# One 128-row read of a head's sums, and the clamp of the weight conversion on GpSimd, in a fused attention and mixer kernel

## The chip, the core and the metric

The kernel runs on one core of one Trainium2 chip. The metric is device time in microseconds (us), here from one launch to its end, as the median of several runs. The engines are named as the profile names them: PE is TensorE, PEld its weight loads, DVE is VectorE, ACT is ScalarE, POOL is GpSimd, SP is SyncE, from whose queue nearly all transfers are issued.

## The reference, cut to what matters

The inputs are q, k and v of shape (8, 8, 576, 64), batch, heads, rows, width, a projection `w_phi` of 64 x 128, and four weights of a mixer in float64. Attention is linear, with 256 features; the mixer works over tokens and then over channels.

```python
def phi(x):
    proj = np.einsum('bhsd,df->bhsf', x, w_phi)
    proj = proj - np.max(np.abs(proj), axis=-1, keepdims=True)
    return np.concatenate([np.exp(proj), np.exp(-proj)], axis=-1)
q_p, k_p = (phi(q), phi(k))
kv = np.einsum('bhsf,bhsd->bhfd', k_p, v)
z = np.sum(k_p, axis=2)
num = np.einsum('bhsf,bhfd->bhsd', q_p, kv)
den = np.einsum('bhsf,bhf->bhs', q_p, z)[..., None] + 1e-06
attn = num / den
...
h = np.maximum(xt @ w_tok1, 0.0) @ w_tok2
u = x + h.transpose(0, 2, 1)
h2 = np.maximum(u @ w_ch1, 0.0) @ w_ch2
return (u + h2).astype(np.float32)
```

## The kernel before, in words

**Streams and the order.** The work is written as five streams: keys (`keys`, line 672), queries (`queries`, 789), the token mix (`token_stream`, 1014), the load and conversion of the mixer's weights (`load_weights`, 568) and the channel mix (`channel_stream`, 1021). Every operation is recorded by a stand-in for the engine (so all of them carry line 175 in the profile), `weave` (1047) gives each a rank, and `arrange` (274) places them: it keeps a clock for each engine, takes the duration of an operation from `cost` (198), adds a lag for its readers, and writes down for each engine one fixed order. On the chip an engine goes through its own list in that order and waits on semaphores. The planner also knows that VectorE and GpSimd can hold each other up (`held`, `choose` at 259): an operation of VectorE that touches no PSUM (`shut`) is placed as if it had to wait for a running operation of GpSimd. GpSimd's operations are costed at 190 ns and 2.1 ns a column.

**Attention.** Heads go in pairs, 32 pairs for the 8 batches; pair i holds two heads j = 0 and 1. The rows of a head are cut into two segments k, of 320 and 256 rows (`SEG`). The first 7 pairs (`PLAIN`) are multiplied in plain f32, the rest in three products of split halves. `less_max` (615) projects, takes the largest absolute value of a row and subtracts it; for split pairs it copies one half out of PSUM (`part`), adds the other into `p` on VectorE, reduces, and lets GpSimd subtract. `turn` (823) transposes the result with TensorE into one PSUM tile `pt` of three blocks of 128 columns and takes the exponentials (`qf`, `qh`, `ql`).

**The numerators.** `numerators` (850) multiplies them with the keys' sums into a PSUM tile `pn` of 128 rows: for head j the 64 rows from 64 j on are the numerator, the other 64 rows are the denominator, one value repeated. Both are read out separately: ScalarE copies the numerator's rows into the attention's result `xt` (`x`), and the denominator's rows go, with 1e-6 added, into `den`, by ScalarE for the first 7 pairs and by VectorE for the other 25. For k = 0 and j = 1 the columns lie in another order, so that each of the two reads is split in two (`runs`). After j = 1 the denominators go through memory: two rows to `row`, back as a small tile `few`, VectorE's reciprocal, out to `inv`, and back by two transfers that repeat each row over 64 partitions of `den`; then GpSimd multiplies `xt` by `den`, in place. The branch for `i >= EARLY` is never taken, as there are 32 pairs and `EARLY` is 32. `den` has two buffers; three `rest` banks of PSUM are shared by `pt`, `pn` and others.

**The conversion.** `convert` (542) makes two f32 halves of a piece of float64 weights, 31 pieces in all, 24 of them 128 x 512 (`bitsc`, `wc`). ScalarE takes the absolute value of the upper word into `m`, VectorE clamps it, shifts it, and joins sign and lower bits in two more operations, ScalarE rounds to the upper half, GpSimd subtracts for the lower half. `m` comes from a ring of three buffers (`bits`). The token weights (7 pieces) come first, the channel weights (24 pieces) after.

**The mixer.** `token_mix` (903) transposes `xt` (`px`), multiplies (`pa`, `ph`) and adds back; `up_proj` and `down_proj` (971, 986) multiply with the channel weights (`h`, `acc`), and `leave` adds and stores.

Of the kernel before, what the change touches and what calls it, by code (L numbers as in the profile page):

```python
# [8 lines left out]
F32 = mybir.dt.float32  # L9
F32R = mybir.dt.float32r  # L10
U32 = mybir.dt.uint32
I64 = mybir.dt.int64
AF = mybir.ActivationFunctionType
ALU = mybir.AluOpType
# [3 lines left out]
P = 128  # L18
B, H, S, D = 8, 8, 576, 64
NP = H // 2  # L20
F = 128
# [4 lines left out]
PLAIN = 7  # L26
OPEN = 4
EARLY = 32
# [449 lines left out]
def mixer_kernel(ctx, tc, qk, qkp, vals, w_phi, w1, w1t, w2, wc1, wc2d, out):  # L478
# [41 lines left out]
    eps = odd.tile([P, 1], F32, tag="eps", name="eps", bufs=1)  # L520
    nc.gpsimd.memset(eps, 1e-6)
# [20 lines left out]
    def convert(hi, lo, src, name, tag=None):  # L542
# [13 lines left out]
        nc.vector.tensor_scalar(m.bitcast(F32), m.bitcast(F32), LEAST, MOST, op0=ALU.max, op1=ALU.min)  # L556
# [58 lines left out]
    def less_max(ts, units, name, base=None):  # L615
# [21 lines left out]
        if base is None:  # L637
            part = wk.tile([P, 2, F], F32, tag="part", name=f"part{name}")
            nc.scalar.copy(part[:, :n], ps[:, :n, 1])
            pr = wk.tile([P, 2, F], F32, tag="p", name=f"p{name}")  # L640
            nc.vector.tensor_tensor(pr[:, :n], ps[:, :n, 0], part[:, :n], op=ALU.add)
            pr, eng = pr[:, :n], nc.gpsimd
        else:
            pr, eng = ps[:, :n, 0], nc.vector
        mx = odd.tile([P, 2], F32, tag=f"mx{kind}", name=f"mx{name}")
# [177 lines left out]
    def turn(i, k, j, pm, tail):  # L823
        w = SEG[k][1]
        ptr = ps_w.tile([P, 3, P], F32, **REST, name=f"pt{i}_{k}{j}")
        rows = [pm[:, 0], pm[:, 1]]
        if k == 0:
            rows.insert(2 * (1 - j), tail[:, 0])
        for n, r in enumerate(rows):
            nc.tensor.transpose(ptr[:, n], r, ident)  # L830

        o = D if k == 0 and j == 1 else 0
        src = ptr.rearrange("p u s -> p (u s)")[:, o:o + w]
        qps = []
        for sg in range(2):
# [5 lines left out]
            hi = st.tile([P, 384], F32R, tag="qh", name=f"qh{i}_{k}{j}{sg}")[:, :w]  # L841
            lo = st.tile([P, 384], F32R, tag="ql", name=f"ql{i}_{k}{j}{sg}")[:, :w]
# [5 lines left out]
    dens, xts = {}, {}  # L848

    def numerators(i, k, j, qps):  # L850
        b, p = divmod(i, NP)
        if b not in xts:
            xts[b] = [wk.tile([P, NC_, SEG[0][1]], F32, tag="xt0", name=f"xt0_{b}", bufs=3),
                      wk.tile([P, NC_, SEG[1][1]], F32, tag="xt1", name=f"xt1_{b}", bufs=3)]
        x = xts[b][k][:, p]
        w = SEG[k][1]
        if j == 0:
            dens[0] = odd.tile([P, SEG[0][1]], F32, tag="den", name=f"den{i}_{k}")[:, :w]
        den = dens[0]
# [7 lines left out]
        rows, drows = slice(j * D, j * D + D), slice(D - j * D, P - j * D)  # L867
        runs = [(0, w, 0)] if not (k == 0 and j == 1) else [(0, D, 256), (D, 256, 0)]
        for a, n, c in runs:
            nc.scalar.copy(x[rows, c:c + n], pn[rows, a:a + n])  # L870
            if i < PLAIN:
                nc.scalar.activation(den[rows, c:c + n], pn[drows, a:a + n], AF.Identity, bias=eps[rows])
            else:
                nc.vector.tensor_scalar(den[rows, c:c + n], pn[drows, a:a + n], 1e-6, None, op0=ALU.add)
        if j == 1:
            if i < EARLY:

                row, inv = (dr.tile([2, w], F32, tag=t, name=f"{t}{i}_{k}") for t in ("row", "inv"))
                few = odd.tile([P, 8], F32, tag="few", name=f"few{i}_{k}")[:, :w // D]
                for r in range(2):  # L880
                    nc.sync.dma_start(row[r:r + 1], den[r * D:r * D + 1])
                nc.sync.dma_start(few, row.rearrange("r (p c) -> (r p) c", c=w // D))
                nc.vector.reciprocal(few, few)
                nc.sync.dma_start(inv.rearrange("r (p c) -> (r p) c", c=w // D), few)
# [249 lines left out]
```

## Time and profile before

| what | us |
| --- | --- |
| median of 3 runs | 1125.2 |
| lowest and highest of them | 1122.74, 1129.52 |
| the profiled execution's own time | 1126.01 |
| its span, first to last instruction | 1124.1 |

The profile is of one execution. Its span is 1.9 us shorter than the time of that execution. A group in the profile is a set of instructions with the same engine, operation and tiles; the tile names leave out buffer numbers and digits, so `bitsc` is `m` of a channel weight, `bits` that of a token weight, `wc` and `wc_l` the halves. "Busy" is the union of the instructions' times, and a mean is of one instruction. The granted clock is given as a share of full speed; it is 1.00 in every stretch.

### The profile page before, as it was taken

To read this page: it belongs to the slowest core of one execution; us is meant where nothing else is said; L and a number is where in the kernel's file an instruction comes from. 1 tells how busy PE (TensorE), PEld (TensorE's weight loads), DVE (VectorE), ACT (ScalarE), POOL (GpSimd) and SP (SyncE) were. 2 spreads that over 40 slices of the span, in tenths; PEclk is the share of its full clock that TensorE was granted. 3 is DMA by queue.
4 is the path that set the end of the run, shared out by engine and by line. 5 is a ranking of instruction groups with operands and counts; after the bars stand their busy time and mean duration, and the time that the engine had idled before them with its cause. 6 is when DMAs were issued, how large, how long until landed. Compare 5 with 4: busy or idle time off the path is not lost.

```text
span 1124.1 us, 24086 instructions
## 1 busy us (share of the span) xinstructions
PE 1087.0 (97%) x8862; PEld 1024.3 (91%) x8862; DVE 702.0 (62%) x1560; ACT 629.2 (56%) x1749; POOL 540.4 (48%) x675
## 2 busy tenths in 40 slices
PE   7999888999999999999999999999999999999998
PEld 7888887898999899999999999999999999999998
DVE  6888888777767666666667765766676655211111
ACT  5877565766666566665756665666665555111110
POOL 0232538666656566565646656665664554011110
PEclk9999999999999999999999999999999999999999
DMA  5645431112121111212122111212121111000000
GB/s 175 157 127 163 150 106 64 50 43 59 31 64 45 46 52 38 64 45 64 41 60 49 43 45 37 67 33 64 45 64 40 32 23 31 12 20 20 20 20 20
DMA packets 60166, 65.42 MB, mean 58 GB/s; under 512 B 27344, under 2 KB 47056, under 8 KB 60048
## 3 DMA queue, kind: packets, MB, share of 16 engines
q1 hardware_dynamic: 59744, 63.48, 20.7%
q8 instruction: 70, 1.15, 0.5%
q14 instruction: 48, 0.39, 0.1%
q10 hardware_dynamic: 304, 0.40, 0.1%
HBM read 54.12 MB, written 9.73 MB: 57 GB/s over the span
## 4 chain that ended last, share of the span: by engine, by line
PE 75%; DMA 10%; DVE 6%; POOL 3%; ACT 3%; issue 2%; SPq 1%; POOLq 0%; ACTq 0%; DVEq 0%
PE acc L175 22%; PE h L175 21%; PE pn L175 7%; PE pkv L175 7%; PE pa L175 4%; DMA den<-inv 4%; PE ppk L175 3%; PE ph L175 3%; DMA inv<-few 3%; PE ppq L175 2%; PE pt L175 2%; DVE bitsc L175 2%; DMA few<-row 2%; PE px L175 1%; DMA row<-den 1%
## 5 line engine op out<-in xcount | busy, mean ns | idle before, releaser
L175 PE MATMUL acc<-gh,wc 128*128 128x256 f32 x1728 | 332.2, 280 | 1.3 <-ACT gh L175 0.7
L175 PEld LDWEIGHTS acc<-gh,wc 128*128 128x128 f32 x1728 | 273.8, 188 | 3.6 <-issue 1.9
L175 PE MATMUL h<-uh,wc_h 128*128 128x256 f32 x864 | 243.0, 281 | 3.1 <-DVE pmq L175 1.6
L175 PE MATMUL h<-uh,wc_l 128*128 128x256 f32 x864 | 242.6, 281 | 0.7 <-POOL wc_l L175 0.7
L175 PE MATMUL h<-ul,wc_h 128*128 128x256 f32 x864 | 241.8, 280 | 0.0
L175 PE MATMUL acc<-gl,wc 128*128 128x256 f32 x864 | 241.4, 280 | 0.0
L175 PEld LDWEIGHTS h<-uh,wc_h 128*128 128x128 f32 x864 | 162.8, 188 | 4.4 <-ACT wc L175 1.7
L175 PEld LDWEIGHTS h<-uh,wc_l 128*128 128x128 f32 x864 | 162.7, 188 | 1.3 <-POOL wc_l L175 0.9
L175 DVE SCALAR_TENSOR_TENSOR gl<-h,gh 128x512 fp32r<-128x512 f32 x108 | 74.4, 689 | 142.8 <-ACT gh L175 142.0
L175 PEld LDWEIGHTS acc<-gl,wc 128*128 128x128 f32 x864 | 162.8, 188 | 0.8 <-issue 0.8
L175 PEld LDWEIGHTS h<-ul,wc_h 128*128 128x128 f32 x864 | 162.7, 188 | 0.3 <-POOL ul L175 0.2
L175 ACT ACTIVATE gh<-h 128x512 fp32r<-128x512 f32 x108 | 64.6, 598 | 139.7 <-PE h L175 139.0
L175 ACT ACTIVATE kp<-pmk 128x256 f32<-128x256 f32 (+1 forms) x320 | 108.2, 390 | 28.2 <-DVE pmk L175 11.6
L175 POOL TENSOR_TENSOR ul<-xt,uh 128x64 fp32r<-128x64 f32 (+3 forms) x120 | 62.2, 549 | 116.3 <-ACT uh L175 115.8
L175 POOL TENSOR_TENSOR ql<-qf,qh 128x320 fp32r<-128x320 f32 (+1 forms) x100 | 83.7, 837 | 67.5 <-ACT qh L175 59.6
L175 ACT ACTIVATE qf<-pt 128x256 f32<-128x256 f32 (+1 forms) x256 | 103.4, 412 | 15.5 <-PE pt L175 13.8
L175 ACT COPY xt<-pn 64x256 f32<-64x256 f32 (+2 forms) x160 | 53.1, 345 | 98.0 <-DVE den L175 72.2
L175 POOL TENSOR_TENSOR pmk<-pk,mxk 128x256 f32<-128x256 f32 (+1 forms) x125 | 80.2, 646 | 46.9 <-DVE mxk L175 32.7
L175 POOL TENSOR_TENSOR xt<-xt,den 128x256 f32<-128x256 f32 (+1 forms) x64 | 53.6, 838 | 95.9 <-DMA den<-inv 88.4
L175 PE MATMUL pn<-qh,kv 128*128 128x320 f32 (+1 forms) x400 | 97.4, 296 | 0.3 <-DVE xl L175 0.3
L175 POOL TENSOR_TENSOR stq<-raw,stq 64x512 fp32r<-64x512 f32 (+1 forms) x50 | 75.2, 1503 | 37.3 <-ACT stq L175 32.5
L175 POOL TENSOR_TENSOR pmq<-pq,mxq 128x256 f32<-128x256 f32 x100 | 64.3, 645 | 51.6 <-DVE mxq L175 42.6
(112 smaller groups left out, 2432.4 us busy)
## 6 DMA issues: line engine op xcount, KB each, us to landing
raw<-in_qk SPq DMA_DIRECT2D x24, 576.0 KB
rawc<-in_wc SPq DMA_DIRECT2D x24, 512.0 KB
v<-in_vals SPq DMA_DIRECT2D x31, 325.0 KB
den<-inv SPq DMA_DIRECT2D x64, 80.0 KB
den<-inv SPq DMA_DIRECT2D x64, 64.0 KB
out_x<-xt SPq DMA_DIRECT2D x12, 256.0 KB
out_x<-xt SPq DMA_DIRECT2D x16, 192.0 KB
pair<-in_qkp SPq DMA_DIRECT2D x7, 320.0 KB
```

The costliest lines, as they stand in the source:

```text
L175: return getattr(getattr(nc, self.unit), self.name)(*[real(a) for a in self.args], **{k: real(v) for k, v in self.kw.items()})
```

## The change

The two reads of `pn` become one of all 128 rows into a new tile `u0` or `u1`, with a two-column bias that adds 1e-6 to the denominator's rows and 0 to the numerator's. ScalarE reads for j = 0, and for j = 1 of the first 7 pairs; VectorE reads for j = 1 of the other 25. The transfers take the denominators from `u0` and `u1` and write the repeated reciprocals over them, and GpSimd multiplies `u0` by `u1` into `xt`, which is written first there. In `turn` the short block of head 1 goes to columns 192 to 319 ahead of the others, so that the columns of both heads have the same order and `runs` is not needed. The branch that was never taken goes. In `less_max` the sum is written over `part`, which gets three buffers in place of two of `part` and two of `p`; one more tile (`mxt`) gets one buffer and `qh` and `ql` lose unused columns. In `convert` the clamp is issued by GpSimd, and the rest stays. The order of all lists is made anew by the same planner.

```diff
--- before.py
+++ after.py
@@ -25,7 +25,6 @@
 NC_, NE, NT = C // P, E // P, T // P
 PLAIN = 7
 OPEN = 4
-EARLY = 32
 WIDE = 104
 BORROWED = 18
 STAGES = 4
@@ -517,8 +516,10 @@
     make_identity(real, ident.made())
     ones = cst.tile([P, D], F32, name="ones")
     nc.gpsimd.memset(ones, 1.0)
-    eps = odd.tile([P, 1], F32, tag="eps", name="eps", bufs=1)
-    nc.gpsimd.memset(eps, 1e-6)
+    eps = odd.tile([P, 2], F32, tag="eps", name="eps", bufs=1)
+    for j in range(2):
+        nc.gpsimd.memset(eps[D - j * D:P - j * D, j:j + 1], 1e-6)
+        nc.gpsimd.memset(eps[j * D:j * D + D, j:j + 1], 0.0)
     wp2 = st.tile([P, 2, F], F32R, tag="wp2", name="wp2", bufs=1)
     wp = cst.tile([P, 2, F], F32, name="wp")
     for j in (1, 0):
@@ -553,7 +554,7 @@
         m = wk.tile([P, 512], U32, tag="bits", name=f"bits{name}", bufs=3)[:w, :n]
 
         nc.scalar.activation(m.bitcast(F32), top.bitcast(F32), AF.Abs)
-        nc.vector.tensor_scalar(m.bitcast(F32), m.bitcast(F32), LEAST, MOST, op0=ALU.max, op1=ALU.min)
+        nc.gpsimd.tensor_scalar(m.bitcast(F32), m.bitcast(F32), LEAST, MOST, op0=ALU.max, op1=ALU.min)
         nc.vector.tensor_scalar(m, m, 3, 0x3FFFFFF8, op0=ALU.logical_shift_left, op1=ALU.bitwise_and)
         nc.vector.scalar_tensor_tensor(m, top, 0xC0000000, m, op0=ALU.bitwise_and, op1=ALU.bitwise_or)
         nc.vector.scalar_tensor_tensor(m, low, 29, m, op0=ALU.logical_shift_right, op1=ALU.bitwise_or)
@@ -635,14 +636,14 @@
             else:
                 nc.tensor.matmul(ps[:, i, 0], t[:, c:c + P], wp[:, base // D], start=True, stop=True)
         if base is None:
-            part = wk.tile([P, 2, F], F32, tag="part", name=f"part{name}")
+            part = wk.tile([P, 2, F], F32, tag="part", name=f"part{name}", bufs=3)
             nc.scalar.copy(part[:, :n], ps[:, :n, 1])
-            pr = wk.tile([P, 2, F], F32, tag="p", name=f"p{name}")
-            nc.vector.tensor_tensor(pr[:, :n], ps[:, :n, 0], part[:, :n], op=ALU.add)
-            pr, eng = pr[:, :n], nc.gpsimd
+            nc.vector.tensor_tensor(part[:, :n], ps[:, :n, 0], part[:, :n], op=ALU.add)
+            pr, eng = part[:, :n], nc.gpsimd
         else:
             pr, eng = ps[:, :n, 0], nc.vector
-        mx = odd.tile([P, 2], F32, tag=f"mx{kind}", name=f"mx{name}")
+        mx = odd.tile([P, 2], F32, tag=f"mx{kind}", name=f"mx{name}",
+                      bufs=1 if kind == "t" else 2)
         nc.vector.tensor_reduce(mx[:, :n], pr, axis=AX.X, op=ALU.max, apply_absolute_value=True)
         pm = wk.tile([P, 1 if kind == "t" else 2, F], F32, tag=f"pm{kind}", name=f"pm{name}",
                      bufs=1 if kind == "t" else 2)
@@ -822,15 +823,13 @@
 
     def turn(i, k, j, pm, tail):
         w = SEG[k][1]
-        ptr = ps_w.tile([P, 3, P], F32, **REST, name=f"pt{i}_{k}{j}")
-        rows = [pm[:, 0], pm[:, 1]]
+        ptr = ps_w.tile([P, 3 * P], F32, **REST, name=f"pt{i}_{k}{j}")
+        at = [(0, pm[:, 0]), (P, pm[:, 1])]
         if k == 0:
-            rows.insert(2 * (1 - j), tail[:, 0])
-        for n, r in enumerate(rows):
-            nc.tensor.transpose(ptr[:, n], r, ident)
-
-        o = D if k == 0 and j == 1 else 0
-        src = ptr.rearrange("p u s -> p (u s)")[:, o:o + w]
+            at.insert(2 * (1 - j), (2 * P - j * D, tail[:, 0]))
+        for c, r in at:
+            nc.tensor.transpose(ptr[:, c:c + P], r, ident)
+        src = ptr[:, :w]
         qps = []
         for sg in range(2):
             full = odd.tile([P, SEG[0][1]], F32, tag="qf", name=f"qf{i}_{k}{j}{sg}")[:, :w]
@@ -838,25 +837,18 @@
             if i < PLAIN:
                 qps.append(full)
                 continue
-            hi = st.tile([P, 384], F32R, tag="qh", name=f"qh{i}_{k}{j}{sg}")[:, :w]
-            lo = st.tile([P, 384], F32R, tag="ql", name=f"ql{i}_{k}{j}{sg}")[:, :w]
+            hi = st.tile([P, SEG[0][1]], F32R, tag="qh", name=f"qh{i}_{k}{j}{sg}")[:, :w]
+            lo = st.tile([P, SEG[0][1]], F32R, tag="ql", name=f"ql{i}_{k}{j}{sg}")[:, :w]
             nc.scalar.activation(hi, src, AF.Exp, scale=1.0 - 2.0 * sg)
             (nc.gpsimd if sg else nc.vector).tensor_tensor(lo, full, hi.bitcast(F32), op=ALU.subtract)
             qps.append((hi, lo))
         return i, k, j, qps
 
-    dens, xts = {}, {}
+    both, xts = {}, {}
 
     def numerators(i, k, j, qps):
         b, p = divmod(i, NP)
-        if b not in xts:
-            xts[b] = [wk.tile([P, NC_, SEG[0][1]], F32, tag="xt0", name=f"xt0_{b}", bufs=3),
-                      wk.tile([P, NC_, SEG[1][1]], F32, tag="xt1", name=f"xt1_{b}", bufs=3)]
-        x = xts[b][k][:, p]
         w = SEG[k][1]
-        if j == 0:
-            dens[0] = odd.tile([P, SEG[0][1]], F32, tag="den", name=f"den{i}_{k}")[:, :w]
-        den = dens[0]
         pn = ps_w.tile([P, SEG[0][1]], F32, **REST, name=f"pn{i}_{k}{j}")[:, :w]
         for sg in range(2):
             w_hl = [kv[:, sg, 2 * j:2 * j + 2].rearrange("p z d -> p (z d)") for kv in kvs[i]]
@@ -864,29 +856,27 @@
                 nc.tensor.matmul(pn, w_hl[0], qps[sg], start=sg == 0, stop=sg == 1)
             else:
                 mm3(pn, w_hl, qps[sg], sg == 0, sg == 1)
-        rows, drows = slice(j * D, j * D + D), slice(D - j * D, P - j * D)
-        runs = [(0, w, 0)] if not (k == 0 and j == 1) else [(0, D, 256), (D, 256, 0)]
-        for a, n, c in runs:
-            nc.scalar.copy(x[rows, c:c + n], pn[rows, a:a + n])
-            if i < PLAIN:
-                nc.scalar.activation(den[rows, c:c + n], pn[drows, a:a + n], AF.Identity, bias=eps[rows])
-            else:
-                nc.vector.tensor_scalar(den[rows, c:c + n], pn[drows, a:a + n], 1e-6, None, op0=ALU.add)
+        u = odd.tile([P, SEG[0][1]], F32, tag=f"u{j}", name=f"u{j}_{i}_{k}")[:, :w]
+        if j == 0 or i < PLAIN:
+            nc.scalar.activation(u, pn, AF.Identity, bias=eps[:, j:j + 1])
+        else:
+            nc.vector.tensor_scalar(u, pn, eps[:, 1:], None, op0=ALU.add)
+        both[j] = u
         if j == 1:
-            if i < EARLY:
-
-                row, inv = (dr.tile([2, w], F32, tag=t, name=f"{t}{i}_{k}") for t in ("row", "inv"))
-                few = odd.tile([P, 8], F32, tag="few", name=f"few{i}_{k}")[:, :w // D]
-                for r in range(2):
-                    nc.sync.dma_start(row[r:r + 1], den[r * D:r * D + 1])
-                nc.sync.dma_start(few, row.rearrange("r (p c) -> (r p) c", c=w // D))
-                nc.vector.reciprocal(few, few)
-                nc.sync.dma_start(inv.rearrange("r (p c) -> (r p) c", c=w // D), few)
-                for r in range(2):
-                    nc.sync.dma_start(den[r * D:(r + 1) * D], inv[r:r + 1].to_broadcast([D, w]))
-            else:
-                nc.vector.reciprocal(den, den)
-            nc.gpsimd.tensor_tensor(x, x, den, op=ALU.mult)
+            if b not in xts:
+                xts[b] = [wk.tile([P, NC_, SEG[0][1]], F32, tag="xt0", name=f"xt0_{b}", bufs=3),
+                          wk.tile([P, NC_, SEG[1][1]], F32, tag="xt1", name=f"xt1_{b}", bufs=3)]
+            x, (u0, u1) = xts[b][k][:, p], (both[0], both[1])
+            row, inv = (dr.tile([2, w], F32, tag=t, name=f"{t}{i}_{k}") for t in ("row", "inv"))
+            few = odd.tile([P, 8], F32, tag="few", name=f"few{i}_{k}")[:, :w // D]
+            nc.sync.dma_start(row[:1], u0[D:D + 1])
+            nc.sync.dma_start(row[1:], u1[:1])
+            nc.sync.dma_start(few, row.rearrange("r (p c) -> (r p) c", c=w // D))
+            nc.vector.reciprocal(few, few)
+            nc.sync.dma_start(inv.rearrange("r (p c) -> (r p) c", c=w // D), few)
+            nc.sync.dma_start(u1[:D], inv[:1].to_broadcast([D, w]))
+            nc.sync.dma_start(u0[D:], inv[1:].to_broadcast([D, w]))
+            nc.gpsimd.tensor_tensor(x, u0, u1, op=ALU.mult)
             if k == sides(i)[1]:
                 attended.add(i)
```

## Rows read from the trace of the kernel before

**Rows 1.** The page, part 1: busy time of TensorE, share of the span, instructions.
```profile
PE 1087.0 (97%) x8862; PEld 1024.3 (91%) x8862; DVE 702.0 (62%) x1560; ACT 629.2 (56%) x1749; POOL 540.4 (48%) x675
```

**Rows 2.** Busy time in four stretches; each engine's busy us, with its instructions in brackets.
```profile
0.00:28.10 28.10, 21.11 (x150) 20.05 (x151) 17.47 (x48) 14.11 (x36) 2.44 (x11) 1.00 0.59 175
28.10:196.70 168.60, 152.52 (x1112) 135.36 (x1112) 141.77 (x296) 117.90 (x303) 72.28 (x68) 1.00 0.45 128
196.70:983.50 786.80, 776.74 (x6399) 732.43 (x6400) 518.11 (x1177) 476.80 (x1364) 453.05 (x572) 1.00 0.18 46
983.50:1124.10 140.60, 136.62 (x1206) 136.43 (x1204) 24.60 (x41) 20.35 (x48) 12.60 (x24) 1.00 0.07 20
```

**Rows 3.** The chain that ended last, from 30 to 205 us, shares by line.
```profile
by line: DVE bitsc L175 12.4%; DMA den<-inv 9.5%; DMA inv<-few 8.3%; issue 5.9%; PE pkv L175 5.6%; DMA few<-row 5.2%; PE acc L175 4.3%; PE pn L175 4.3%; PE ppk L175 3.6%; PE h L175 3.6%; PE pa L175 3.3%; DMA row<-den 2.8%; SPq L175 2.7%; PO
```

**Rows 4.** Waits of TensorE, 28 to 200 us: total us, times, longest.
```profile
PE ppk L175 <- DVE pmk L175: 2.6, 3, 1.4
PE px L175 <- POOL xt L175: 2.0, 3, 1.2
PE h L175 <- DVE pmq L175: 1.6, 1, 1.6
PE ph L175 <- DVE xt L175: 1.1, 2, 0.6
```

**Rows 5.** Groups by shape: the conversion (busy us, mean ns, idle before).
```profile
L175 DVE TENSOR_SCALAR bitsc<-bitsc 128x512 f32<-128x512 f32 x24 | 15.1, 630 | 2.3 <-ACT bitsc L175 2.3
L175 DVE TENSOR_SCALAR bits<-bits 128x512 f32<-128x512 f32 x2 | 0.8, 417 | 0.0
L175 POOL TENSOR_TENSOR wc_l<-bitsc,wc_h 128x512 fp32r<-128x512 f32 x12 | 15.9, 1331 | 22.1 <-ACT wc_h L175 22.1
```

**Rows 6.** Timeline, 126.6 to 128.9 us: start us, us, engine, what.
```profile
126.64 0.68 DVE L175 SCALAR_TENSOR_TENSOR bitsc<-rawc,bitsc 128x512 uint32<-128x512 uint32 x1
...
127.12 2.79 POOL L175 TENSOR_TENSOR wc_l<-bitsc,wc_h 128x512 fp32r<-128x512 f32 x2 [2.49 <-ACT wc_h L175]
...
127.25 1.51 DVE L175 TENSOR_SCALAR bitsc<-bitsc 128x512 uint32<-128x512 uint32 x1
```

**Rows 7.** Groups by shape: GpSimd's instructions with one input or none.
```profile
masks.py:199 POOL TENSOR_SCALAR_AFFINE_SELECT ident<-ident 128x128 f32<-128x128 f32 x1 | 0.3, 295 | 0.1
masks.py:197 POOL MEMSET ident<- 128x128 f32 x1 | 0.2, 205 | 0.3 <-POOLq L1121 0.3
L175 POOL MEMSET ones<- 128x64 f32 x1 | 0.2, 152 | 0.0
```

**Rows 8.** Groups of instructions, shapes together: reading the sums out of PSUM.
```profile
L175 ACT COPY xt<-pn 64x256 f32<-64x256 f32 (+2 forms) x160 | 53.1, 345 | 98.0 <-DVE den L175 72.2 <-PE pn L175 23.6
L175 DVE TENSOR_SCALAR den<-pn 64x256 f32<-64x256 f32 (+2 forms) x125 | 48.1, 394 | 45.0 <-PE pn L175 35.5 <-ACT xt L175 6.1 <-DMA den<-inv 1.3
L175 ACT ACTIVATE den<-pn,eps 64x256 f32<-64x256 f32 (+2 forms) x35 | 15.5, 447 | 6.8 <-POOL xt L175 6.3
```

**Rows 9.** Groups by shape: durations for the reads of PSUM by width.
```profile
L175 ACT ACTIVATE den<-pn,eps 64x320 f32<-64x320 f32 x7 | 3.7, 527 | 4.1 <-POOL xt L175 4.0
L175 ACT ACTIVATE den<-pn,eps 64x256 f32<-64x256 f32 x21 | 9.8, 467 | 2.6 <-POOL xt L175 2.3
L175 DVE TENSOR_SCALAR den<-pn 64x320 f32<-64x320 f32 x25 | 12.3, 493 | 10.9 <-PE pn L175 9.3 <-ACT xt L175 1.1
L175 DVE TENSOR_SCALAR den<-pn 64x256 f32<-64x256 f32 x75 | 31.4, 419 | 24.4 <-PE pn L175 19.0 <-ACT xt L175 2.9 <-DMA den<-inv 1.3
L175 ACT COPY xt<-pn 64x256 f32<-64x256 f32 x96 | 35.1, 366 | 56.3 <-DVE den L175 43.2 <-PE pn L175 11.9
L175 ACT COPY partk<-ppk 128x256 f32<-128x256 f32 x100 | 37.4, 374 | 54.8 <-PE ppk L175 52.1 <-DVE pq L175 1.1 <-DVE den L175 0.5
```

**Rows 10.** Waits of ScalarE, 28 to 200 us: total us, times, longest.
```profile
ACT den L175 <- POOL xt L175: 6.3, 6, 2.4
```

**Rows 11.** Waits of GpSimd, 28 to 200 us: total us, times, longest.
```profile
POOL xt L175 <- DMA den<-inv: 30.2, 12, 4.8
POOL wc_l L175 <- ACT wc_h L175: 22.1, 9, 5.2
```

## The prediction

> **What bounds the kernel now.** I read the busy times first. TensorE is busy for 97% of the span and no other engine for more than 62% [rows 1], so an edit that takes no work from TensorE can only win back time in which TensorE waits. This change leaves its products and transposes as they are. The stretches show where it waits [rows 2]: it is idle for 168.6 - 152.5 = 16.1 us from 28 to 197 us, for 10.1 us of the 787 us after that, for 7.0 us in the start-up before 28 us, and for 4.0 us at the end. Records of pipelined products hide short gaps, so the true waits are somewhat more, but some 26 us in the two middle stretches is the size of what can be had.
>
> In the stretch from 28 to 197 us VectorE is busy for 141.8 us, 84%, ScalarE for 70% and GpSimd for 43% [rows 2]. The reader should see that VectorE is nearly full there and that GpSimd has 96 us free. The chain of waits says the same: VectorE's steps of the weight conversion are its largest item, 12.4%, and the transfers of the denominators, written as den, inv, few and row, come to 25.8% together [rows 3]. Of the four longest waits of TensorE in this stretch three end with VectorE, 5.3 us, and one with GpSimd's product into xt, 2.0 us [rows 4]. After 197 us VectorE is busy for 66% and ScalarE for 61% [rows 2].
>
> **The clamp.** VectorE loses the 24 large clamps, 24 x 0.630 = 15.1 us [rows 5]. The seven small ones come mostly before the stretch that matters and are not counted. GpSimd gains them. No row shows a clamp on GpSimd. Below, a fill of 64 columns takes 152 ns and one of 128 columns 205 ns, 0.83 ns a column, so 512 columns take 205 + 384 x 0.83 = 524 ns; above, the subtraction of two 128x512 inputs takes 1331 ns [rows 5, 7]. I take the one-input row, 295 ns for 128 columns, and add 384 x 0.83: an estimate of 0.61 us [rows 7], 24 x 0.61 = 14.7 us on an engine with 96 us free.
>
> The two engines hold each other up, however. The same clamp takes 417 ns for a token weight in the start-up, where GpSimd is busy for 2.4 of 28 us [rows 2], and 630 ns on average among the channel weights [rows 5], and a shift that began 0.13 us into GpSimd's subtraction took 1.51 us, while an operation of two inputs before it took 0.68 us [rows 6]. So a clamp on GpSimd can stop VectorE for as much as it lasts. I charge half of 0.61 us, since VectorE is not always in an operation that is stopped: 24 x 0.31 = 7.3 us, with 0 and 14.7 us as ends. With the upper price of 1.33 us the charge at half is 16 us, and nothing is left. Net, VectorE is freed of 15.1 - 7.3 = 7.8 us. As it is the fullest engine and the one that ends most of TensorE's waits there, I pass on two thirds: **-5 us**. The ends, with no charge and with a full one, are -10 and 0 us.
>
> The Trainium skill's page GPSIMD Engine Reference, section Engine selection, says that an elementwise operation with one input runs there at about line rate. Its figure of 1.03 cycles an element at 1.2 GHz gives an estimate of 0.44 us for 512 columns without the start of the instruction; by it the charge would be 5.3 us and this term -6.5 us. No run here shows it.
>
> The hand-over adds a wait. VectorE's shift now waits for GpSimd's clamp, and behind that shift, in VectorE's fixed order, stand the maxima and subtractions that TensorE waits for. In GpSimd's order the clamp stands among products into xt that wait for the denominators' transfers: 30.2 us in 12 waits [rows 11]. I cost this at nothing because a conversion has three tiles of m in flight and the planner costs the clamp at 190 + 2.1 x 512 = 1265 ns, twice my estimate, and so leaves VectorE's shift late enough. If that cover is gone, it is the rival that ends slower.
>
> **One read of the sums.** Before, ScalarE copies 160 times and adds 1e-6 35 times, and VectorE adds it 125 times [rows 8]. After, there are 128 reads: 64 for j = 0 and 14 for j = 1 on ScalarE, 50 on VectorE. Rows and not columns double, and the time goes by columns: a copy of 64x256 takes 366 ns, one of 128x256 374 ns [rows 9]. ScalarE's reads with a bias take 527 and 467 ns for 320 and 256 columns, VectorE's 493 and 419 ns [rows 9]. VectorE's bias now comes from a tile rather than a constant; no row shows this form, and I take the constant's price, the nearest. Below lies ScalarE's copy without a bias, 366 ns for 256 columns, -1.3 us over 25 reads; above, ScalarE's read with a bias tile, 527 and 467 ns, +2.1 us over 50. Neither moves the sum.
>
> - The first 7 pairs, on ScalarE: 35 copies of 345 ns are 12.1 us and 35 additions of 447 ns are 15.6 us; in their place 14 x 527 + 14 x 467 ns = 13.9 us. ScalarE is freed of 13.8 us. It is 70% busy and ends none of the four waits [rows 2, 4], so I pass on 1 us, with 0 and 3 as ends: **-1 us**.
> - The other 25 pairs: ScalarE has 125 x 345 ns = 43.1 us before and 25 x (527 + 467) ns = 24.9 us after, VectorE 125 x 394 ns = 49.3 us before and 25 x (493 + 419) ns = 22.8 us after. That is 18.2 and 26.5 us out of 787 us, and with it goes a wait of 72.2 us in which ScalarE stands still for VectorE's read of the same tile [rows 8]. Engines that are a third idle gain little by it; what they can give is part of TensorE's 10.1 us. I take a third: **-3 us**, with 0 and 6 as ends.
>
> **Edits that I cost at nothing.** The transfers of a pair and segment stay at six, in the same order on SP's queue, so their round trip stays. GpSimd's product keeps its width and waits for the same transfers, and the two u tiles have two buffers as den had, so the wait of 6.3 us for a free one [rows 10] stays as well. TensorE transposes the same three blocks; that the short one comes first is hidden by the two behind it. The sum over part is the same operation, on a ring of three where there were two of each; if ScalarE came to wait for GpSimd there, the price is one copy, 0.37 us [rows 9], now and then. The extra fills at the start are of the size of the 152 ns row [rows 7], on an idle engine in the start-up; uncovered they cost 0.5 us. The branch that goes was never taken.
>
> **The sum** is -5 - 1 - 3 = -9 us against this execution's own 1126.0 us, thus 1117.0. The median of the runs lies 0.8 us below this execution, so I forecast **1116 us**. With the ends of the first term, -14 and -4 us, the forecast's own range is 1111 to 1121 us.
>
> **The rivals.**
>
> *VectorE behind GpSimd's waits (slower).* The place is GpSimd's list during the conversion, wherever a clamp stands behind a product into xt that waits for den<-inv. Then VectorE's shift starts late by the rest of that wait, 2.5 us on average [rows 11], and all behind it. For it: VectorE is 84% busy there, with little to take a delay in; the planner's costs for transfers are fixed, while these waits reach 4.8 us. Against: GpSimd is idle often, and three tiles are in flight. It decides from 6 of the 12 waits on, as 6 x 2.5 us = 15 us eats the 15.1 us that the clamp frees. With all 12, VectorE is 30.2 - 15.1 = 15.1 us worse off; half of that on TensorE is +7.5 us, 1133 us. Chance 0.18.
>
> *The engines hold each other up in full (no change).* Each clamp on GpSimd stops VectorE for its whole length, 24 x 0.61 = 14.7 us against 15.1 us freed [rows 5, 7], and only the reads of the sums are left, -4 us: 1121.5 us, rounded 1122. For it, the shift of 1.51 us [rows 6]; against it, the operation of two inputs at 0.68 us, which shows that VectorE is not always in the way. Chance 0.15. The Trainium skill, page SBUF — State Buffer, section SBUF: two separate sides, has this as a rule: the port pair that VectorE and GpSimd share is an exclusive lock held for the whole instruction, and the other fully blocks. By that rule the trace agrees for the shift of 1.51 us.
>
> *The transfers set the pace (no change).* In the stretch to 197 us the denominators' transfers are 25.8% of the chain [rows 3], with two buffers, and nothing about them changes. Then a freed VectorE only waits longer. I give it -2 us, 1124 us. For it, the wait for a free den [rows 10]; against it, that TensorE waits 2.0 us for xt and more for VectorE [rows 4]. Chance 0.14.
>
> *VectorE was the whole of it (faster still).* All 15.1 us pass to TensorE, and half of the 10.1 us later: -20 us, 1105 us. Against it, GpSimd's hold. Chance 0.13.
>
> **How the numbers follow.** The forecast keeps 0.40. A measurement of this kernel can tell about 0.5%, 5.6 us, from no change. Faster by more are the forecast and the last rival, 0.53; within are the two that change nothing, 0.29; slower is the first, 0.18. The range of 1104 to 1131 us takes in the forecast's bounds, both cases without change, half of the fastest and the milder half of the slowest.
>
> **What would show it.** Right: VectorE's busy time from 28 to 197 us some 8 us or more lower, TensorE's idle time there near 10 us, ScalarE's wait for VectorE at pn gone, some 128 reads of about 0.37 to 0.53 us, clamps on GpSimd near 0.6 us. Wrong: clamps near 1.3 us, VectorE waiting for GpSimd's bitsc for more than 15 us in total, other operations of the conversion longer than before by what the clamp freed, or the last piece of weights converted later than before.

## The result: 12 us faster, and the profile after

The changed kernel takes 1112.87 us (median of 4 runs, 1110.0 to 1115.77) against 1125.24 us before: a ratio of 0.9889, 95% interval 0.9859 to 0.9919. Four runs in a later session gave 1113.36 us and 0.9898 (0.9880 to 0.9915). The profiled execution took 1115.77 us, its span is 1113.9 us.

The stretches answer to [rows 2]; the two later bounds are moved, so that the last one again holds the channel mix alone. Columns are stretch, length, and busy us of TensorE, its weight loads, VectorE, ScalarE and GpSimd, with the instructions of each in brackets, then the granted clock, the share of the DMA engines and GB/s.

```profile
0.00:28.10 28.10, 20.90 (x156) 19.71 (x157) 17.21 (x47) 13.92 (x36) 8.88 (x18) 1.00 0.59 175
28.10:196.70 168.60, 150.13 (x1082) 136.48 (x1080) 127.67 (x258) 101.00 (x251) 121.39 (x94) 0.97 0.44 124
196.70:973.00 776.30, 770.93 (x6423) 731.64 (x6423) 503.43 (x1111) 459.28 (x1298) 458.18 (x575) 1.00 0.18 47
973.00:1113.90 140.90, 136.92 (x1209) 136.72 (x1207) 24.59 (x41) 20.67 (x49) 12.53 (x24) 1.00 0.07 20
```

TensorE is idle for 18.5 us from 28 to 197 us, where some 10 were forecast and 16.1 us were lost before, although VectorE lost 14 us of work and ScalarE 17 us there. After that it is idle for 5.4 us instead of 10.1 us. So the gain does not lie in the stretch that the clamp was to relieve. The granted clock, 1.00 there before, has a mean of 0.97: three times, from 118, 169 and 180 us on, it is at 0.50, its lower level, for 3.4 us.

Idle time tells only a part of the gain, however. The page after has, in its part 1:

```profile
PE 1078.9 (97%) x8862; PEld 1024.5 (92%) x8862; DVE 672.9 (60%) x1454; ACT 594.9 (53%) x1632; POOL 601.0 (54%) x709
```

TensorE's busy time fell from 1087.0 us [rows 1] to 1078.9 us with the same 8862 products, and its idle time only from 37.1 to 35.0 us. So 8.1 of the 10.2 us by which the span is shorter lie in what the profile counts as busy: the ends of pipelined products are modelled there, so that short waits between products can hide in it; no run took them apart. The number of products started in a stretch shows the place better. From 28 to 197 us it is 1082 against 1112 before, and the gain comes after 300 us, where no weights are converted (300 to 960 us, before and after):

```profile
300.00:960.00 660.00, 652.29 (x5406) 618.38 (x5405) 434.16 (x995) 402.85 (x1154) 385.81 (x489) 1.00 0.18 47
300.00:960.00 660.00, 657.10 (x5513) 628.84 (x5513) 427.23 (x949) 392.25 (x1107) 393.71 (x495) 1.00 0.19 48
```

107 products more are some 12 us, at about 0.115 us each.

The groups that answer to [rows 5] and [rows 8], shapes together (busy us, mean ns, idle time before and what ended it):

```profile
L174 POOL TENSOR_SCALAR bitsc<-bitsc 128x512 f32<-128x512 f32 x24 | 49.2, 2059 | 12.2 <-ACT bitsc L174 12.2
L174 DVE SCALAR_TENSOR_TENSOR bitsc<-rawc,bitsc 128x512 uint32<-128x512 uint32 x48 | 41.8, 885 | 0.4
L174 ACT ACTIVATE u<-pn,eps 128x256 f32<-128x256 f32 (+1 forms) x78 | 38.5, 501 | 44.3 <-PE pn L174 34.4 <-POOL pmq L174 5.2 <-POOL xt L174 3.6
L174 DVE TENSOR_SCALAR u<-pn,eps 128x320 f32<-128x320 f32 (+1 forms) x50 | 25.7, 514 | 23.6 <-PE pn L174 18.3 <-POOL xt L174 3.1 <-DMA u<-inv 1.3
L174 DVE TENSOR_SCALAR bitsc<-bitsc 128x512 uint32<-128x512 uint32 x24 | 18.6, 776 | 8.4 <-POOL bitsc L174 8.3
```

The clamp takes 2.06 us on GpSimd, more than three times my estimate and above the end of 1.33 us. The tile's own row (shortest, median and longest in ns, first and last start) speaks against contention as what makes it long: half of them lie within 9 ns of the shortest.

```profile
L174 POOL TENSOR_SCALAR bitsc<-bitsc x24: 1907/1916/2467, 46.8 to 170.4; 128x512 f32<-128x512 f32 x24
```

The time of the conversion's tile bitsc by engine, 28 to 200 us (VectorE, ScalarE, GpSimd), first before and then after:

```profile
28.00:200.00 172.00, 69.10 (x96) 29.90 (x48) 33.08 (x24) 1.00 0.44 127
```

```profile
28.00:200.00 172.00, 59.56 (x72) 30.44 (x48) 81.49 (x48) 0.97 0.44 125
```

VectorE is freed of 9.5 us, and GpSimd pays 48 us. And VectorE waits for the late clamps, a wait that was not there before (waits of VectorE, 28 to 200 us: total, times, longest):

```profile
DVE bitsc L174 <- POOL bitsc L174: 8.3, 8, 1.8
```

The clamp on GpSimd now heads the chain of waits from 30 to 205 us, where VectorE's conversion did before [rows 3]:

```profile
by line: POOL bitsc L174 10.4%; PE h L174 8.5%; PE pkv L174 5.9%; DVE bitsc L174 5.7%; DMA inv<-few 5.6%; PE pn L174 5.5%; PE acc L174 5.3%; DMA few<-row 4.8%; POOL wc_l L174 4.6%; issue 4.3%; PE ppk L174 4.2%; POOL wc L174 4.1%; PE ppq L17
```

9.5 us freed and 8.3 us waited: the clamp as a part of its own looked worth nothing. That the whole is 12 us faster asked for the parts one by one.

### The profile page after: what moved, and what is told of

Read it like the earlier page. It is cut to its first block, busy times and chain, and to the rows that moved or that the text cites. A ratio compares the mean times of both kernels' runs of the same rounds, so it can differ in the third digit from the quotient of the medians.

```text
span 1113.9 us, 23838 instructions
## 1 busy us (share of the span) xinstructions
PE 1078.9 (97%) x8862; PEld 1024.5 (92%) x8862; DVE 672.9 (60%) x1454; ACT 594.9 (53%) x1632; POOL 601.0 (54%) x709
## 4 chain that ended last, share of the span: by engine, by line
PE 82%; DMA 7%; POOL 4%; DVE 3%; issue 1%; ACT 1%; SPq 0%; ACTq 0%; POOLq 0%; DVEq 0%
PE h L174 24%; PE acc L174 24%; PE pn L174 7%; PE pkv L174 7%; PE pa L174 4%; PE ph L174 4%; PE ppk L174 4%; PE ppq L174 3%; DMA u<-inv 3%; PE pt L174 3%; DMA inv<-few 2%; POOL bitsc L174 2%; PE px L174 1%; DMA few<-row 1%; DVE bitsc L174 1%
## 5 line engine op out<-in xcount | busy, mean ns | idle before, releaser
L174 POOL TENSOR_TENSOR ul<-xt,uh 128x192 fp32r<-128x192 f32 (+3 forms) x120 | 61.1, 541 | 119.4 <-ACT uh L174 118.9
L174 POOL TENSOR_TENSOR pmk<-partk,mxk 128x256 f32<-128x256 f32 (+1 forms) x125 | 84.9, 684 | 55.8 <-DVE mxk L174 35.1
L174 POOL TENSOR_TENSOR xt<-u,u 128x256 f32<-128x256 f32 (+1 forms) x64 | 54.2, 847 | 82.3 <-DMA u<-inv 80.6
L174 POOL TENSOR_TENSOR stk<-raw,stk 64x512 fp32r<-64x512 f32 (+1 forms) x50 | 71.7, 1447 | 41.7 <-ACT stk L174 39.7
L174 ACT ACTIVATE qh<-pt 128x320 fp32r<-128x320 f32 (+1 forms) x200 | 84.7, 424 | 0.1
```

The source lines that it names most:

```text
L174: return getattr(getattr(nc, self.unit), self.name)(*[real(a) for a in self.args], **{k: real(v) for k, v in self.kw.items()})
```

## The experiments

Each run stands beside runs of the kernel before on the same chip. Theory A is the forecast; theory B, formed on the profile after, says that the clamp gives nothing and the reads give all; theory C says that the planner's new order does it.

**The reads without the clamp.** The changed kernel, with

```diff
-        nc.gpsimd.tensor_scalar(m.bitcast(F32), m.bitcast(F32), LEAST, MOST, op0=ALU.max, op1=ALU.min)
+        nc.vector.tensor_scalar(m.bitcast(F32), m.bitcast(F32), LEAST, MOST, op0=ALU.max, op1=ALU.min)
```

> The changed kernel with the clamp back on VectorE, so that only the reads of the sums and the tiles that go with them are changed. Theory A (my forecast: the clamp gives 5 us and the reads 4): about 1118 us. Theory B (the clamp on GpSimd takes 1.92 us and gives nothing; the whole gain of 12 us is from the reads, after 197 us): 1113 us or less, 1108 us if the clamp costs what the stretch before 197 us seems to have lost. Theory C (the gain comes from the order that the planner wrote anew, not from any edit): anywhere from 1110 to 1130 us.

Measured: 1113.95 us, ratio 0.9916 (0.9891 to 0.9940). Against 0.9889 and 0.9898 with the clamp on GpSimd the intervals overlap: in the changed kernel the clamp's place makes no difference that can be told. The 5 us that the forecast gave it are not there.

The equal times hide a difference by stretch. With the clamp on VectorE TensorE starts 1136 products from 28 to 197 us, 54 more than the changed kernel, and is idle for 11.0 us in place of 18.5 us:

```profile
28.10:196.70 168.60, 157.62 (x1136) 140.10 (x1135) 142.05 (x301) 106.60 (x267) 71.28 (x71) 0.98 0.44 129
```

So the clamp on GpSimd does cost time there, some 6 us. The changed kernel has it back by the end, in part because this run's last products are slow by some 6 us, as told at the end; but a run without that was no faster.

**The clamp without the rest.** The opposite edit, made to the kernel before.

> The kernel before with the clamp on GpSimd and nothing else. Theory A: 1120 us, TensorE idle for less than 16.1 us from 28 to 197 us. Theory B: 1125 to 1132 us, no less idle time of TensorE there, since VectorE waits for clamps of 1.92 us. Theory C: 1115 to 1130 us whatever the clamp does.

Measured: 1152.19 us, ratio 1.0238 (1.0216 to 1.0259): 27 us slower, beyond what theory B expected. Stretch from 28 to 197 us, and the wait from 28 to 200 us:

```profile
28.10:196.70 168.60, 143.13 (x1013) 127.72 (x1013) 122.85 (x245) 108.72 (x273) 112.42 (x85) 0.98 0.43 119
```

```profile
DVE bitsc L175 <- POOL bitsc L175: 13.5, 13, 2.9
```

TensorE is idle for 25.5 us there, 9.4 us more than before, and starts 1013 products in place of 1112. The same edit is worth -1 us in one kernel and +27 us in the other, so the parts don't add.

**The sum over part, alone.** The kernel before, with

```diff
-            part = wk.tile([P, 2, F], F32, tag="part", name=f"part{name}")
+            part = wk.tile([P, 2, F], F32, tag="part", name=f"part{name}", bufs=3)
             nc.scalar.copy(part[:, :n], ps[:, :n, 1])
-            pr = wk.tile([P, 2, F], F32, tag="p", name=f"p{name}")
-            nc.vector.tensor_tensor(pr[:, :n], ps[:, :n, 0], part[:, :n], op=ALU.add)
-            pr, eng = pr[:, :n], nc.gpsimd
+            nc.vector.tensor_tensor(part[:, :n], ps[:, :n, 0], part[:, :n], op=ALU.add)
+            pr, eng = part[:, :n], nc.gpsimd
```

> The kernel before with the sum written over part, in a ring of three, and nothing else. Theory A costs this edit at nothing: 1125 us. A rival to it says that the ring of three is what shortens the stretch after 197 us: 1116 us or less.

Measured: 1117.01 us, ratio 0.9936 (0.9914 to 0.9958). An edit that I cost at nothing gives 8 us.

**The order, nudged.** The kernel before with `HOLD = 126.0` in place of 120.0.

> The kernel before with one constant of the planner (the hold between VectorE and GpSimd, 120 ns) set to 126 ns: the same operations, in orders that differ from some 45 us on. Theories A and B: within 4 us of 1125 us. Theory C: off by 6 us or more to either side, so that an edit cannot be told from a new order.

Measured: 1126.13 us, ratio 1.0013 (0.9999 to 1.0027). Another order of the same work changes the time by 1 us. Theory C falls for changes of the size seen here, as far as one nudge shows.

**Depth or place.** Two runs on the ring: part with two buffers and p with three as separate tiles (unused columns of qh and ql go as well), and the sum over part with a ring of two.

```diff
-            pr = wk.tile([P, 2, F], F32, tag="p", name=f"p{name}")
+            pr = wk.tile([P, 2, F], F32, tag="p", name=f"p{name}", bufs=3)
```

> The kernel before with part and p left as two tiles, part with two buffers and p with three (unused columns of qh and ql are dropped to make room). If the depth of the ring that GpSimd's subtraction frees is what gave the 8 us of the run with the sum written over part: 1117 us. If it was the writing in place, or a shorter wait of ScalarE for part: 1125 us.

> The kernel before with the sum written over part in a ring of two instead of three, so one buffer fewer in all. If depth is the cause, slower than the ring of three by more than 8 us: 1126 us or more. If writing in place is the cause: 1117 us.

Measured: 1121.51 us, ratio 0.9968 (0.9953 to 0.9983), and 1141.97 us, ratio 1.0151 (1.0130 to 1.0173). From a ring of two to one of three in place it is 25 us, so in place depth decides; but the separate tiles with three p give under half of the 8 us, and what gives the rest is open. The waits over the whole run show the ring. In the kernel before, VectorE's sum waits for GpSimd to give back p:

```profile
DVE pk L175 <- POOL pmq L175: 5.6, 6, 2.5
DVE pk L175 <- POOL pmk L175: 2.7, 3, 1.2
```

with two in place ScalarE's copy waits instead:

```profile
ACT partk L175 <- POOL pmk L175: 7.2, 9, 1.5
ACT partk L175 <- POOL pmq L175: 5.0, 6, 1.4
```

and with three there is one such wait for partk:

```profile
ACT partk L175 <- POOL pmq L175: 2.2, 1, 2.2
```

**The changed kernel without the reads.** The diff of the sum over part and the clamp on GpSimd, both on the kernel before.

> The changed kernel without the new reads: the kernel before with the sum over part in a ring of three and the clamp on GpSimd. If the clamp's loss of 27 us adds to the gain of 8 us: 1144 us. If the ring of three takes up GpSimd's lateness: 1117 us, and the reads have no part in that. Between them, 1125 to 1140 us, would say that the ring helps and the reads are needed as well.

Measured: 1146.25 us, ratio 1.0188 (1.0164 to 1.0211): the clamp's loss is there in full, 29 us on top of 1117 us. The ring does not make up for it; the reads, with the tiles that come with them, do, for they take this kernel to 1113 us. About half of the loss has come up by 197 us, with 1009 products started where the kernel without the clamp, part alone, has 1123. The other half comes from 197 to 300 us, 706 against 828 products, and its place is seen in the chain of waits from 255 to 290 us of this run (start us, us, what):

```profile
268.21 2.73 PE pa L175 x11
...
270.96 0.61 ACT ah L175
...
271.60 0.70 DVE al L175
...
272.34 1.88 PE ph L175 x11
...
278.41 1.36 PE h L175 x12
```

That is the token mix, step after step, with no product of the channel mix beside it. As I read it, the channel mix has used up the first batch and waits for the second. Busy time of the products into acc in the same run (TensorE, loads, VectorE, then the clock) is nothing for 20 us, and the granted clock has means of 0.74 and 0.92, between its two levels, 1.2 and 2.4 GHz:

```profile
250.00:260.00 10.00, 3.26 (x24) 2.95 (x24) 1.51 (x4) 1.00 0.31 88
260.00:270.00 10.00, 0.00 (x0) 0.00 (x0) 0.00 (x0) 0.74 0.05 13
270.00:280.00 10.00, 0.00 (x0) 0.00 (x0) 0.00 (x0) 0.92 0.20 62
```

All engines' rows show what came before the clock fell. TensorE was busy for 2.36 of 4.70 us, and then the clock was at its lower level for nearly all of 6.9 us:

```profile
260.00:264.70 4.70, 2.36 (x12) 1.30 (x11) 4.37 (x10) 4.09 (x14) 3.35 (x5) 1.00 0.11 28
264.70:271.60 6.90, 6.35 (x26) 5.77 (x26) 3.85 (x11) 2.25 (x8) 3.38 (x5) 0.51 0.00 0
```

In the changed kernel the hole is less than half as long, and the clock stays:

```profile
250.00:260.00 10.00, 0.00 (x0) 0.00 (x0) 0.38 (x1) 1.00 0.22 56
260.00:270.00 10.00, 0.50 (x2) 0.39 (x3) 0.00 (x0) 1.00 0.19 46
```

The Trainium skill's page TensorE: Matmul & The Clock Gate, section What's actually happening, says that the clock is throttled by default and that activity lifts it; the row of 0.51 behind the half-busy one agrees. Such a hole so costs more than TensorE's idle time in it: eleven products into pa took 2.73 us at the lower clock, 248 ns each, where twelve took 1.59 us, 133 ns each, in the kernel before at 491 us.

**The single read.** The changed kernel with the clamp on VectorE, and u read in two halves:

```diff
-        if j == 0 or i < PLAIN:
-            nc.scalar.activation(u, pn, AF.Identity, bias=eps[:, j:j + 1])
-        else:
-            nc.vector.tensor_scalar(u, pn, eps[:, 1:], None, op0=ALU.add)
+        rows, drows = slice(j * D, j * D + D), slice(D - j * D, P - j * D)
+        nc.scalar.copy(u[rows], pn[rows])
+        if i < PLAIN:
+            nc.scalar.activation(u[drows], pn[drows], AF.Identity, bias=eps[drows, j:j + 1])
+        else:
+            nc.vector.tensor_scalar(u[drows], pn[drows], 1e-6, None, op0=ALU.add)
```

> The changed kernel with the clamp on VectorE and with u read out of PSUM in two halves of 64 rows again, the numerator by ScalarE and the denominator by ScalarE (first 7 pairs) or VectorE, so that tiles, column order and transfers are the new ones and only the number of reads is the old one. The single read itself is what keeps the attention ahead: 1117 us or more, near the run with the sum over part alone, and the mix of the second batch later than at 250 us. The gain lies in the new tiles or the new order: 1114 us.

Measured: 1128.88 us, ratio 1.0040 (1.0024 to 1.0055), 15 us above the same kernel with one read. The wait is back, on the other engine: VectorE stands still for ScalarE's read of the same tile, 42.8 us in all.

```profile
L174 ACT COPY u<-pn 64x256 f32<-64x256 f32 (+1 forms) x128 | 50.4, 393 | 87.0 <-PE pn L174 69.2 <-issue 6.5 <-POOL xt L174 4.3
L174 DVE TENSOR_SCALAR u<-pn 64x320 f32<-64x320 f32 (+1 forms) x100 | 45.4, 454 | 47.3 <-ACT u L174 42.8 <-DMA u<-inv 1.9 <-POOL pmq L174 1.2
```

So it is the one read in place of two, and not the tiles or the order of columns, that gives against this run. It also shows that the new tiles by themselves are no gain: with two reads this run is 12 us slower than the sum over part alone.

**The planner told the truth.** The changed kernel with the measured cost of the clamp in `cost`:

```diff
+    if op.name == "tensor_scalar":
+        return 190 + 3.4 * n
     return 190 + 2.1 * n
```

> The changed kernel with the planner's cost of a clamp on GpSimd set to 190 ns + 3.4 ns a column, 1931 ns for 512 columns, instead of 1265 ns; the operations are the same. If VectorE's waits behind late clamps cost the changed kernel time: 1105 to 1110 us. If the clamps are covered as they stand: 1113 us.

Measured: 1127.19 us, ratio 1.0021 (1.0008 to 1.0034): a miss, 14 us slower than with the wrong cost. VectorE waits less for clamps, 5.2 us, but the last weights come 10 us later and TensorE is idle for 23.9 us from 28 to 197 us:

```profile
28.10:196.70 168.60, 144.74 (x1009) 130.84 (x1009) 119.20 (x246) 95.25 (x237) 112.40 (x86) 0.94 0.42 121
```

**The clamp twice.** The changed kernel with the clamp's line repeated; the values stay.

> The changed kernel with the clamp done twice on GpSimd (the second leaves the values as they are), 24 x 1.92 us = 46 us more on GpSimd. If the clamp is harmless in the changed kernel only because the attention of the second batch still ends before the channel mix runs out of work: 1135 us or more, with TensorE going without channel products for 20 us near 260 us, as in the two slow runs. If GpSimd's time is free in the changed kernel: 1113 to 1118 us.

Measured: 1148.45 us, ratio 1.0214 (1.0195 to 1.0232). GpSimd's time is not free in the changed kernel; the next 46 us of it cost 35 us. The place is only partly the one expected: VectorE waits for clamps for 26.1 us from 28 to 200 us, and the weights themselves come late, the last at 243 us; TensorE has started 934 products in place of 1082 by 197 us, and 651 in place of 797 from there to 300 us.

**The changed kernel again.**

> The changed kernel once more, to stand beside the others of this call: 1113 us, 0.5% or more below the kernel before. It tells whether the clamp on GpSimd is worth anything against the run with it on VectorE, 1114 us: below 1110 us it is, above 1116 us it costs.

Measured: 1113.36 us, between the two bounds: the clamp's place is worth nothing here that can be told.

**The reads without the clamp, in another order.** The first run of this study with `HOLD = 126.0`, for a reason told at the end.

> The changed kernel with the clamp on VectorE, as in the first run of this study, and the planner's hold at 126 ns. In that first run TensorE's products followed each other at 117.7 ns instead of 113.3 ns from 942 us to the end, some 6 us. If that pace is an accident of the order, another order ends at 113.3 ns and at 1108 us, so that the clamp on GpSimd costs the changed kernel 5 us. If it comes with the clamp on VectorE, or if the new order loses elsewhere: 1114 us.

Measured: 1114.21 us, ratio 0.9908 (0.9889 to 0.9926). The products ended at 113.3 ns, and the time was the same: what one order loses at the end, the other loses elsewhere. This order, too, starts more products from 28 to 197 us than the changed kernel, 1141 against 1082.

Numbers from each run's profile put them side by side: when GpSimd begins the last lower half of the weights, the hole, which is the longest time between two starts of products into h or acc from 220 to 280 us, and the products of any kind that TensorE starts in three stretches (28.1 to 196.7, to 300, to 960 us).

| kernel | us | last weights, us | hole, us | to 197 | to 300 | to 960 |
| --- | --- | --- | --- | --- | --- | --- |
| before | 1125 | 181 | 7.9 | 1112 | 801 | 5406 |
| clamp on GpSimd alone | 1152 | 196 | 20.3 | 1013 | 699 | 5392 |
| part alone | 1117 | 178 | 5.4 | 1123 | 828 | 5455 |
| part in a ring of two | 1142 | 182 | 24.1 | 1104 | 726 | 5356 |
| part and clamp, no reads | 1146 | 198 | 24.0 | 1009 | 706 | 5442 |
| changed, clamp on VectorE | 1114 | 176 | 5.6 | 1136 | 823 | 5485 |
| the same with two reads | 1129 | 179 | 18.2 | 1122 | 744 | 5428 |
| changed | 1113 | 186 | 10.9 | 1082 | 797 | 5513 |
| changed, planner told | 1127 | 196 | 11.0 | 1009 | 790 | 5510 |
| changed, clamp twice | 1148 | 243 | 15.7 | 934 | 651 | 5541 |

100 products are some 11 to 12 us. The clamp puts the last weights back by 10 to 20 us, and wherever it went to GpSimd TensorE falls behind before 197 us, by 54 products in the changed kernel and by 99 and 114 in the two with the old reads. The five holes of 15 us or more in this window belong to the five slowest kernels, and no other goes beyond 11 us. In the stretch that holds the hole the ring of two and the two reads lose most of their products, 75 and 79, and the two kernels with the clamp and the old reads lose another 102 and 122. Planner told loses its time before 197 us and has no such hole.

The hole is a sign and no measure of the loss: from 254 to 278 us of part and clamp TensorE is busy with other products for 19.4 of 23.9 us, and part alone, which is fast, has a time of 15.0 us without a channel product at 366 us, outside this window. My reading is that late weights cost a second time when the second batch's attention is not ready as the first batch's channel work runs out. No run moved the token mix of the second batch alone, so this is argued from ten profiles and not isolated. Two kernels were not tried: the reads with the two old rings of two, and a ring of four.

## Why the prediction was right, and where it was not

The total held: -9 us was forecast and -12 us measured, inside 1104 to 1131 us. That was luck in good part, since by its own steps the prediction was less good. Of the signs that it named, TensorE's idle time from 28 to 197 us was 18.5 us and not near 10 us, the clamps took 2.06 us and not 0.6 us, and the last weights came later, at 186 us and not 181 us. VectorE's lower busy time, by 14.1 us, and the signs of the reads came out.

- **What could be had.** "An edit that takes no work from TensorE can only win back time in which TensorE waits" holds, but the size, "some 26 us" of idle time, left out the waits hidden in busy time, which the prediction named and then did not count. 8.1 of the 10.2 us by which the span fell lie in busy time.
- **The price of the clamp on GpSimd** failed. The estimate of 0.61 us from a one-input row was 2.06 us, 1.91 us at its shortest; even the end of 1.33 us, a subtraction of two inputs, was too low. A clamp has two arithmetic steps and the rows that I took have none or one selection; whether that is the reason was not tried. The Trainium skill's page GPSIMD Engine Reference, section Engine selection, calls one-input operations there "roughly line-rate"; the prediction's estimate beside it was 0.44 us. For this instruction the measurement decides against both.
- **The charge for the engines holding each other up**, 7.3 us, was about twice too high in the changed kernel. With the clamps on GpSimd the shift went from 674 to 776 ns and the joins from 860 to 885 ns, 24 x 0.10 + 48 x 0.025 = 3.6 us. VectorE was freed of 9.5 us, where I had 7.8. The groups by shape of the kernel before, beside those of after above:

```profile
L175 DVE SCALAR_TENSOR_TENSOR bitsc<-rawc,bitsc 128x512 uint32<-128x512 uint32 x48 | 40.6, 860 | 0.1
L175 DVE TENSOR_SCALAR bitsc<-bitsc 128x512 uint32<-128x512 uint32 x24 | 16.2, 674 | 0.1
```

- **The hand-over**, "cost at nothing" with three tiles in flight, cost 8.3 us. It took back what was freed. So the term of -5 us was about 0 over the whole run: with the clamp on VectorE it is 1114 us, in the changed kernel 1113 us. In the conversion's own stretch the sign was wrong, by 54 products or some 6 us.
- **The reads**, -4 us. Counts and durations came out: 78 reads on ScalarE at 501 ns (forecast 497) and 50 on VectorE at 514 ns (456). With the sum over part already in place they give 3 us with the clamp on VectorE, but 33 us with the clamp on GpSimd (1146 to 1113 us), and undoing them in the changed kernel with the clamp on VectorE costs 15 us. ScalarE's wait of 72.2 us for VectorE [rows 8] did go. I called the engines a third idle and passed on little. Undone, they cost 79 products from 197 to 300 us, around the hole, and 57 more to 960 us, so mean load was the wrong guide; why the cost falls there is argued above and not shown.
- **The sum over part**, "the same operation, on a ring of three where there were two of each": I saw the ring, priced one wait of 0.37 us for the worse, and did not ask whose release it waits for. It gives 8 us alone, a term that the prediction put at nothing.
- **The rivals.** The first, slower by VectorE behind GpSimd, is what the clamp does by itself, +27 us, and more than its +7.5 us. Its mechanism is only half borne out: VectorE waits for late clamps, but in the changed kernel GpSimd's 12.2 us of idle time just before the clamps end with ScalarE's absolute value, not with a transfer. The net loss did not come about in the changed kernel; the ring alone does not prevent it, so it takes the reads, and how they do it is argued. "The engines hold each other up in full" was not seen: 3.6 us of 14.7. That the transfers set the pace was not tested by itself. It gave 1124 us, and their six transfers stayed while the time fell by 12 us; but most of that came after 300 us, and the rival speaks of the stretch to 197 us, where TensorE gained nothing. There the clamp's place alone moved 54 products, so the transfers were not the only limit.

So the range held because two errors in size cancelled: the clamp gave some 4 to 5 us less than forecast and the ring 8 us more.

## What to carry to other kernels

Measure an instruction on its engine before moving it there; the nearest row by input count can be off by three. In a pipeline of streams with a fixed order, do not price an edit by mean load: the same edit was worth -1 us in one kernel and +27 us in another, and of the 27 us some 11 came up in the stretch of the edit and some 12 where the next stage seems to run out of work. Count what the bounding engine has started by the end of each stretch, since its busy time can hide waits. And ask of each buffer that a change adds or drops which engine gives it back.

## What was not expected of the hardware

TensorE's stretches of equal products, 128x256 at a granted clock of 1.00, follow each other at one of two paces, 113.3 or 117.7 ns, and keep the pace until products of another kind come between. The run with the clamp on VectorE fell into the slower one at 942 us and kept it to the end, some 1400 products, 6 us; the changed kernel ended in the faster. All engines' rows from 1011 to 1039 us, first that run, then the changed kernel; the count of products in the same 28 us shows it:

```profile
1011.00:1039.00 28.00, 28.00 (x240) 28.00 (x239) 4.21 (x7) 4.30 (x9) 2.85 (x4) 1.00 0.07 20
```

```profile
1011.00:1039.00 28.00, 28.00 (x249) 28.00 (x249) 4.97 (x9) 3.72 (x8) 0.24 (x1) 1.00 0.07 20
```

What sets the pace was not found; the nudged order ended at the faster one without being faster in all. The pace has no part in the 12 us: the mean distance of two channel products that follow each other (starts less than 135 ns apart) is 115.2 ns both in the kernel before and in the changed one, and 116.4 ns in the run with the clamp on VectorE.
